# A part of w2 on 64 partitions, loaded by eight transfers of eight rows beside the first eight heads

## The chip, the cores and the metric

The kernel runs on one core of a Trainium2 chip. The metric is device time in microseconds (us), the median of several executions. The core has 16 DMA engines (in the trace, a transfer to 128 partitions closes with 16 tiny packets), and they are what this case is about.

## The reference

It is one decode step: a token of two sequences attends over the last 4096 places of a cache, and beside it runs a small dense layer.

```python
# B=2, Sq=1, D=448, 16 query heads, 8 kv heads, Dh=256, W=4096 of 32768 cached places
# F=1792; all arrays bfloat16
xn = layernorm(x)
q = (xn @ wq)                                   # 448 x 4096
k, v = k_cache[:, :, -W:, :], v_cache[:, :, -W:, :]   # each kv head serves two query heads
o = softmax(q @ k.T * Dh**-0.5) @ v
h = xn @ w1 + b1                                # 448 x 1792
act = h * tanh(softplus(h))                     # Mish
out = x + o @ wo + act @ w2                     # w2 is 1792 x 448, 1.6 MB
```

There are 2 x 8 = 16 "heads" of cache to read, each 2 MB of k and 2 MB of v. With the weights this is 77.67 MB from memory in 188.7 us, and little arithmetic on it.

## The kernel before

All large loads are issued by SyncE (SP) in program order into rotating buffers: four for k, five for v. The dense weights use v buffers before the v tiles do. The parts that the change touches:

```python
b1_sb = consts.tile([1, F], BF16)
nc.scalar.dma_start(out=b1_sb[:, :], in_=B_b1.rearrange("(o f) -> o f", o=1))
# ... cut ...
spread = consts.tile([P, NB, P], BF16)
for b4 in range(NB):                      # 16 small copies, used by experiment e3
    rows = slice(b4 * Q, (b4 + 1) * Q)
    for j in range(NQ):
        nc.vector.tensor_copy(out=spread[rows, b4, j * Q : (j + 1) * Q], in_=ident[rows, rows])
# ... cut ...
def load_dense():
    dense["w1"] = v_tile(NS * HF).rearrange("p (s n) -> p s n", s=NS)
    # ... cut: w1 is loaded ...
    dense["w2"] = v_tile(NX * NF * D).rearrange("p (x c d) -> p x c d", x=NX, c=NF)
    nc.sync.dma_start(                    # NX=2 halves, NF=7 rows of w2 on each of 128 partitions
        out=dense["w2"], in_=B_w2.rearrange("(x q c) d -> q x c d", x=NX, q=P)
    )

def dense_in():                           # h, then Mish, into act_bf
    hT_ps = ps_m.tile([P, NF, NX, Bsz], FP32, tag="m", name="hT_ps")
    for c in range(NF):
        # ... cut: 7 matmuls over w1 and 2 for the bias, for each c ...

def dense_out():                          # act @ w2
    w2_sb = dense.pop("w2")
    for x in range(NX):
        for c in range(NF):
            add(act_bf[:, c, x, :], w2_sb[:, x, c, :])

# ... cut ...
for i in range(NK + KA):                  # NK = 16 heads
    if i + 2 < NK:
        load_k(i + 2)
    if i < NK:
        load_v(i, (0, T) if i < NK - 1 else (0, T // 2, 3 * T // 4, T))
        kvh, b = heads[i]
        if b == Bsz - 1:
            load_wo(kvh, parts=1 if i < NK - 1 else 2)
        # ... cut: two halves of k: transpose, scores, softmax ...
    if i == 0:
        dense_in()
    if i == 1:
        dense_out()
    # ... cut: o = p @ v, @ wo ...
```

The softmax here doesn't subtract the row's maximum and nothing guards it: scores larger than these inputs give would overflow.

## Time and profile before

| | before |
|---|---|
| time, median of the first 3 runs | 190.46 us (190.43 to 190.48) |
| span of the profiled execution | 188.7 us |
| share of the 16 DMA engines' span filled by packets of the main queue | 97.3% |
| TensorE's matmuls, VectorE, ScalarE busy | 76%, 60%, 17% |
| last packet of data ends | 185.03 us |
| last v quarter has landed | 184.27 us |
| output issued | 186.51 us |

The last three rows are times from the start of the span. The strips, the DMA table and the chain of work are shown and read in the prediction. The first line below is from the groups of instructions: VectorE's 32 transposes of k, with busy time and mean nanoseconds, then its idle time before them and what ended it. The other two are from the table of DMA issues: count, size of one, and the median time from issue to landing.

```profile
L364 DVE STREAM_TRANSPOSE kt<-k 128x2048 f32<-128x2048 f32 x32 | 73.4, 2296 | 50.6 <-DMA k<-in_A_k_cache_dram 49.6
...
k<-in_A_k_cache_dram SPq DMA_DIRECT2D x16, 2048.0 KB, 31.5
v<-in_A_v_cache_dram SPq DMA_DIRECT2D x15, 2048.0 KB, 34.8
```

VectorE waits 49.6 us in all for k, so it has time to spare. A tile of k is asked for 31.5 us before it lands, though a head of k and v takes only about 10 us to move: several tiles are queued behind the one that moves. A few issues of SyncE do wait for a free buffer (the longest 6.7 us, for a transpose of k), but the DMA engines have other tiles to move meanwhile.

The strips, which sum up nearly eight thousand packets, do not show that one engine is later than another. For that I took the trace's packet records (start, duration, bytes, queue of each packet), followed the strict chains that they form, and noted when each engine reached the tiny packet that closes a transfer. Such lists of **lateness** (nanoseconds after the first of the 16 engines) are my own working from those records, and stand in ordinary fences.

### The profile page before, as it was taken

Reading aid. Unit: us, or ns where it says so; the run is one execution under the profiler, and the core shown is the slowest. Engines: PE = TensorE matmul, PEld = TensorE weight load, DVE = VectorE, ACT = ScalarE, POOL = GpSimd, SP = SyncE. Lnnn points to the kernel's source line nnn. Section 1 sums busy time; section 2 is a strip of 40 time slices with the busy share of each in tenths; the row PEclk is TensorE's granted clock in tenths of the full one; section 3 lists DMA queues with packets and bytes.
Section 4 is the critical chain, followed back from the end, with each engine's and each line's share of the span. In section 5 each row is a group of like instructions: output and inputs, shape, how many; then the busy total and the mean of one; then the engine's idle time right before and its main releaser. Section 6 shows DMA issues by size and latency. Waiting matters only on the chain.

```text
span 188.7 us, 2944 instructions
## 1 busy us (share of the span) xinstructions
PE 144.1 (76%) x1158; PEld 71.7 (38%) x1158; DVE 113.5 (60%) x195; ACT 32.5 (17%) x82; POOL 27.1 (14%) x139
## 2 busy tenths in 40 slices
PE   0152991788995799869985999769986999597782
PEld 0042390234442345334432434324533443254671
DVE  7805505997919392857649381939376673939401
ACT  2300110112212022111222112202311121211101
POOL 8004430033030022003030203003110300000000
PEclk9999995799999699988999699969998799969955
DMA  6999999999999999999999999999999999999991
GB/s 216 423 432 422 430 430 434 438 431 420 417 441 431 420 416 438 441 427 405 442 434 429 434 420 431 434 431 420 431 431 438 412 432 434 431 441 417 408 394 49
DMA packets 7816, 77.86 MB, mean 413 GB/s; under 512 B 757, under 2 KB 2809, under 8 KB 3322
## 3 DMA queue, kind: packets, MB, share of 16 engines
q1 hardware_dynamic: 7796, 77.66, 97.3%
q8 instruction: 9, 0.15, 0.3%
q14 instruction: 5, 0.04, 0.1%
q10 hardware_dynamic: 6, 0.01, 0.0%
HBM read 77.67 MB, written 0.00 MB: 412 GB/s over the span
## 4 chain that ended last, share of the span: by engine, by line
DMA 82%; DVE 11%; issue 2%; PE 2%; SPq 1%; ACT 0%; ACTq 0%
DMA k<-in_A_k_cache_dram 68%; DMA v<-in_A_v_cache_dram 14%; DVE kt L364 8%; DVE pT L397 2%; PE sc L376 1%; SPq L114 0%; PE psA L214 0%; SPq L338 0%; PE q L479 0%; SPq L280 0%; DVE sums L407 0%; SPq L275 0%; DVE sums L404 0%; DVE den_sb L320 0%; ACT p L386 0%
## 5 line engine op out<-in xcount | busy, mean ns | idle before, releaser
L364 DVE STREAM_TRANSPOSE kt<-k 128x2048 f32<-128x2048 f32 x32 | 73.4, 2296 | 50.6 <-DMA k<-in_A_k_cache_dram 49.6
L376 PE MATMUL sc<-kt,qdiag 128*128 128x512 bf16 x256 | 72.7, 433 | 17.6 <-DVE kt L364 15.8
L376 PEld LDWEIGHTS <-qdiag 128*128 128x128 bf16 x256 | 24.7, 105 | 57.2 <-issue 30.0
L431 PE MATMUL o<-v,pT 128*4 128x512 bf16 x192 | 43.4, 379 | 0.0
L264 POOL COPY qdiag<-qrep 32x8 bf16<-32x8 bf16 x128 | 23.1, 213 | 122.4 <-PE sc L376 107.6
L386 ACT ACTIVATE p<-sc 128x512 bf16<-128x512 f32 x32 | 19.1, 597 | 95.6 <-PE sc L376 93.1
L431 PEld LDWEIGHTS <-pT 128*4 128x4 bf16 x192 | 15.8, 87 | 21.8
L397 DVE STREAM_TRANSPOSE pT<-p 128x512 bf16<-128x512 bf16 x32 | 21.5, 672 | 1.1 <-ACT p L386 1.1
L439 ACT COPY o_sb<-o 4x512 f32<-4x512 f32 x12 | 6.9, 574 | 36.8 <-PE o L431 36.8
L214 PE MATMUL psA<-wo,oT 128*2 128x112 bf16 x128 | 3.8, 245 | 11.0 <-DVE oT L447 11.0
L479 PE MATMUL q<-pT,v 128*128 128x2 bf16 x256 | 7.6, 165 | 1.7 <-DMA v<-in_A_v_cache_dram 1.6
L460 PEld LDWEIGHTS q<-ident_f,o_sb 4*128 4x128 f32 x48 | 6.6, 206 | 5.1 <-issue 5.1
L479 PEld LDWEIGHTS <-v 128*128 128x128 bf16 x256 | 7.3, 101 | 2.0 <-DMA v<-in_A_v_cache_dram 2.0
L414 PEld LDWEIGHTS den<-sums,ones_f 128*128 128x128 f32 x32 | 6.8, 220 | 3.3 <-issue 1.7
L460 PE MATMUL q<-ident_f,o_sb 4*128 4x4 f32 x48 | 7.6, 261 | 0.0
L235 PE MATMUL qT_ps<-xs,v 128*128 128x4 bf16 x112 | 3.3, 166 | 4.8 <-DVE ones L201 2.8
L214 PEld LDWEIGHTS <-oT 128*2 128x2 bf16 x128 | 1.8, 87 | 11.9 <-DVE oT L447 11.7
L386 ACT ACTIVATION_READ_ACCUMULATOR p<-sc 128x1 f32 x32 | 6.2, 194 | 0.0
L177 PE MATMUL xnT_ps<-ident,xn_bf 2*128 2x2 bf16 x7 | 0.5, 167 | 6.3 <-DVE xn_bf L139 6.3
L414 PE MATMUL den<-sums,ones_f 128*128 128x2 f32 x32 | 5.1, 229 | 0.0
L235 PEld LDWEIGHTS <-v 128*128 128x128 bf16 x112 | 3.1, 104 | 5.0 <-issue 3.0
L462 DVE COPY osum<-q 128x4 f32<-128x4 f32 x12 | 1.9, 158 | 3.9 <-PE q L460 3.9
(52 smaller groups left out, 46.5 us busy)
## 6 DMA issues: line engine op xcount, KB each, us to landing
k<-in_A_k_cache_dram SPq DMA_DIRECT2D x16, 2048.0 KB, 31.5
v<-in_A_v_cache_dram SPq DMA_DIRECT2D x15, 2048.0 KB, 34.8
v<-in_B_w_dram SPq DMA_DIRECT2D x2, 1568.0 KB, 21.0
wo<-in_A_wo_dram SPq DMA_DIRECT2D x7, 448.0 KB, 31.5
v<-in_A_wq_dram SPq DMA_DIRECT2D x1, 2048.0 KB
v<-in_A_wq_dram SPq DMA_DIRECT2D x1, 1536.0 KB, 10.8
v<-in_A_v_cache_dram SPq DMA_DIRECT2D x1, 1024.0 KB, 29.1
v<-in_A_v_cache_dram SPq DMA_DIRECT2D x2, 512.0 KB, 27.4
```

What stands on the lines that cost most here:

```text
L214: nc.tensor.matmul(part(n), lhsT=lhsT, rhs=w[:, n * DO : (n + 1) * DO], start=start, stop=stop, tile_position=(0, n * Q), skip_group_check ...
L235: nc.tensor.matmul(qT_ps[:, hh, e, :], lhsT=wq_v[s][:, hh, e, :], rhs=xs[:, s, :, :].rearrange("p x b -> p (x b)"), start=(s == 0), stop=( ...
L264: nc.gpsimd.tensor_copy(out=tv[rows, :, e, j * Q : (j + 1) * Q : HS], in_=qrep[rows, :, h0 : h0 + rep, e, x, b],)
L364: nc.vector.transpose(out=kt[:].bitcast(FP32), in_=k[:, half * TH * Dh : (half + 1) * TH * Dh].bitcast(FP32),)
L376: nc.tensor.matmul(psc[:], lhsT=qdiag[i % NW][:, n * NE + e, :], rhs=ktv[:, n, e, :, :], start=(n == 0 and e == 0), stop=(n == NB - 1 and ...
L386: nc.scalar.activation(out=p_sb[:], in_=psc[:].rearrange("p t c -> p (t c)"), func=ACT.Exp, scale=scale, accum_out=state["rs", i][:, s % N ...
L397: nc.vector.transpose(out=pT[:], in_=p_t.pop(s)[:])
L414: nc.tensor.matmul(den[:], lhsT=ones_f[:], rhs=state.pop(("sums", i))[:], start=True, stop=True)
L431: nc.tensor.matmul(po[:], lhsT=pT_t[i * NH + half][:, uh * NP * Q : (uh + 1) * NP * Q : HS], rhs=v[:, u * NP : (u + 1) * NP, :].rearrange( ...
L439: nc.scalar.copy(out=o_sb[:], in_=po[:])
L460: nc.tensor.transpose(pqv[:, u, c, :], ov[:, u, c, :], ident_f[0:NR, 0:NR])
L479: nc.tensor.matmul(po[:, c, :], lhsT=vv[:, t, c, :], rhs=pTv[:, th, 0:Q:HS], start=(t == 0 and c == 0), stop=(t == T - 1), skip_group_chec ...
```

## The change

The intent, as it can be read from the diff: part of w2 is taken out of the transfer that spreads over 16 engines and given to eight of them, so that those eight carry a little more and the other eight a little less. Six of the seven row groups of each half of w2 stay on 128 partitions (NA = 6). The last 128 rows of each half go, two by two, onto 64 partitions, and come in eight transfers of eight partitions, one beside each of the first eight heads. The eight partitions of a transfer lie four apart.

```diff
-    NF = HF // P
+    PW = P // 2
+    NA = HF // P - 1
+    NF = NA + (HF - P * NA) // PW
 ...
+    w2_rest = consts.tile([PW, NX, NF - NA, D], BF16)
+    def hidden(c):
+        if c < NA:
+            return slice(0, P), slice(c, P * NA, NA)
+        return slice(0, PW), slice(P * NA + c - NA, HF, NF - NA)
 ...  b1 moves into the spare end of w1's v buffer
-        dense["w2"] = v_tile(NX * NF * D).rearrange("p (x c d) -> p x c d", x=NX, c=NF)
+        dense["w2"] = v_tile(NX * NA * D).rearrange("p (x c d) -> p x c d", x=NX, c=NA)
 ...
+    def load_rest(u):
+        q0, j = divmod(u, 4)
+        rows = slice(q0 * Q + j, (q0 + 1) * Q, 4)
+        rest = w2_in[:, P * NA : HF, :].rearrange("x (q c) d -> q x c d", q=PW)
+        nc.sync.dma_start(out=w2_rest[rows, :, :, :], in_=rest[rows, :, :, :])
 ...
         hT_ps = ps_m.tile([P, NF, NX, Bsz], FP32, tag="m", name="hT_ps")
+        nc.vector.memset(hT_ps[:], 0.0)
 ...  the hidden layer's matmuls take rows and columns from hidden(c)
+    def dense_rest():
+        for x in range(NX):
+            for c in range(NA, NF):
+                add(act_bf[0:PW, c, x, :], w2_rest[:, x, c - NA, :])
 ...
+            if i < PW // 8:
+                load_rest(i)
 ...
+        if i == 11:
+            dense_rest()
```

More of the change, by code (lines that the diff above doesn't have):

```diff
@@ L98 @@
     nc.scalar.dma_start(out=x_bf[:, :], in_=A_x.flatten_outer_dims())
-    b1_sb = consts.tile([1, F], BF16)
-    nc.scalar.dma_start(out=b1_sb[:, :], in_=B_b1.rearrange("(o f) -> o f", o=1))
     def v_tile(n):
@@ L270 @@
     act_bf = consts.tile([P, NF, NX, Bsz], BF16)
+    w2_rest = consts.tile([PW, NX, NF - NA, D], BF16)
     dense = {}
+    def hidden(c):
+        if c < NA:
+            return slice(0, P), slice(c, P * NA, NA)
+        return slice(0, PW), slice(P * NA + c - NA, HF, NF - NA)
+    w2_in = B_w2.rearrange("(x f) d -> x f d", x=NX)
     def load_dense():
-        dense["w1"] = v_tile(NS * HF).rearrange("p (s n) -> p s n", s=NS)
+        w = v_tile(NS * HF + F)
+        dense["w1"] = w[:, 0 : NS * HF].rearrange("p (s n) -> p s n", s=NS)
+        dense["b1"] = w[0:1, NS * HF : NS * HF + F]
         nc.sync.dma_start(
@@ L278, in load_dense @@
         )
-        dense["w2"] = v_tile(NX * NF * D).rearrange("p (x c d) -> p x c d", x=NX, c=NF)
+        nc.scalar.dma_start(out=dense["b1"], in_=B_b1.rearrange("(o f) -> o f", o=1))
+        dense["w2"] = v_tile(NX * NA * D).rearrange("p (x c d) -> p x c d", x=NX, c=NA)
         nc.sync.dma_start(
-            out=dense["w2"], in_=B_w2.rearrange("(x q c) d -> q x c d", x=NX, q=P)
-        )
+            out=dense["w2"],
+            in_=w2_in[:, 0 : P * NA, :].rearrange("x (q c) d -> q x c d", q=P),
+        )
+    def load_rest(u):
[3 more added lines that the diff above has]
+        nc.sync.dma_start(out=w2_rest[rows, :, :, :], in_=rest[rows, :, :, :])
     def dense_in():
-        w1_v = dense.pop("w1").rearrange("p s (q c) -> p s c q", c=NF)
-        b1_v = b1_sb[:].rearrange("o (x q c) -> o x c q", x=NX, c=NF)
+        w1, b1 = dense.pop("w1"), dense.pop("b1")
         hT_ps = ps_m.tile([P, NF, NX, Bsz], FP32, tag="m", name="hT_ps")
+        nc.vector.memset(hT_ps[:], 0.0)
         for c in range(NF):
+            rows, cols = hidden(c)
             for s in range(NS):
                 nc.tensor.matmul(
-                    hT_ps[:, c, :, :].rearrange("p x b -> p (x b)"),
-                    lhsT=w1_v[:, s, c, :],
+                    hT_ps[rows, c, :, :].rearrange("p x b -> p (x b)"),
+                    lhsT=w1[:, s, cols],
                     rhs=xs[:, s, :, :].rearrange("p x b -> p (x b)"),
@@ L299, in dense_in @@
                 nc.tensor.matmul(
-                    hT_ps[:, c, x, :],
-                    lhsT=b1_v[:, x, c, :],
+                    hT_ps[rows, c, x, :],
+                    lhsT=b1[:, x * HF + cols.start : x * HF + cols.stop : cols.step],
                     rhs=ones[:, :],
@@ L326, in dense_out @@
         for x in range(NX):
-            for c in range(NF):
+            for c in range(NA):
                 add(act_bf[:, c, x, :], w2_sb[:, x, c, :])
+    def dense_rest():
+        for x in range(NX):
+            for c in range(NA, NF):
+                add(act_bf[0:PW, c, x, :], w2_rest[:, x, c - NA, :])
     NSTEP = len(heads) * NH
```

## The prediction

> **What bounds the kernel now.** I read the page's strips first, then the DMA table, then the chain of work that ended last, then the waits, and last the trace's packet records one by one, because the first four all point at the DMA engines.
>
> ```profile
> PE   0152991788995799869985999769986999597782
> DVE  7805505997919392857649381939376673939401
> DMA  6999999999999999999999999999999999999991
> GB/s 216 423 432 422 430 430 434 438 431 420 417 441 431 420 416 438 441 427 405 442 434 429 434 420 431 434 431 420 431 431 438 412 432 434 431 441 417 408 394 49
> ```
>
> The DMA strip is at nine tenths in 38 of 40 slices and the rate is flat near 430 GB/s; no compute engine is full for long. There is no stretch in which the transfers wait for anyone.
>
> ```profile
> q1 hardware_dynamic: 7796, 77.66, 97.3%
> q8 instruction: 9, 0.15, 0.3%
> q14 instruction: 5, 0.04, 0.1%
> ...
> DMA 82%; DVE 11%; issue 2%; PE 2%; SPq 1%; ACT 0%; ACTq 0%
> ```
>
> 97.3% of 16 engines' whole span is data of the program. The two "instruction" queues look like nothing, but keep them in mind: nine packets of 16 KB and a few of 8 KB, each of which sits on one engine.
>
> The chain of work in order of time, its last part, and the longest wait of VectorE:
>
> ```profile
> 127.28 31.36 DMA k<-in_A_k_cache_dram
> ...
> 158.66 25.61 DMA v<-in_A_v_cache_dram
> 184.27 0.05 issue
> 184.31 0.60 PE q L479 x16
> ...
> 184.94 0.18 DVE oT L447
> ...
> 185.16 0.79 PE psA L214 x15
> ```
>
> ```profile
> DVE kt L364 <- DMA k<-in_A_k_cache_dram: 49.6, 14, 9.0
> ```
>
> So the end is: the last quarter of the last v tile lands at 184.27, then about 2 us of compute and the output. A tile has landed when the last of its DMA engines has delivered, so **the slowest of 16 engines sets the time**, not their mean.
>
> Which engine is slow? The packet records of the trace carry start, duration, size and queue. In the main queue the packets fall into 16 strict chains: a 16384 B packet starts 607 ns after the one before it on its engine (27.0 GB/s). The tiny packets that close a transfer therefore give each engine's lateness, in ns after the first engine. My reading of them:
>
> ```
> at   7.4 us: 0 24 30 63 110 141 149 173 194 195 227 230 284 345 407 594
> at 177.2 us: 0 30 172 345 407 594 | 830 887 | 1483 1529 1561 1567 1614 1642 1647 | 1694
> ```
>
> At first the spread is 0.6 us and its order stays exactly the same until an instruction packet comes. After the 16 KB packet of queue 8 at 17.1 us the engine at 227 is at 1647; after the one at 61.7 us the one at 63 is at 1483, and so on: each such packet costs its engine 1.42 us, and each of the seven so far took a different engine. An eighth, at 180.0 us, moves the engine at 0 to 1422. The 8 KB packets of queue 14 cost 0.5 to 0.9 us; four fell during the loads, and two of those (at 48.7 and 175.7 us) on the same engine, which so became the last of all, at 1694. At the end there are seven early engines (up to 888), eight late ones (1422 to 1647) with one fetch each, and that one at 1694.
>
> [...] The trace agrees for 128 rows (16 closing packets per transfer) and for the one-row bias (one packet, at 5.77 us); no transfer of eight is in it. [...]nine packets of 16384 B for 2338 records on TensorE's two rows, about one per 256. [...] The bias's engine[...] can be followed through its exact start times: it is the one at 345, so it is an early one.
>
> **The change part by part.**
>
> Intent, as I read it: the eight engines that carry one TensorE fetch each are 8 to 15, so let the other eight carry a bit more. Seven engines fit that; the eighth does not.
>
> *Main part of w2.* Still two rows' groups on 128 partitions, 16 packets per engine, but 5376 B in place of 6272 B. A 6272 B packet takes a step of 235 ns (239 in the records less 4 of overlap); in proportion 5376 B is 201. Saved: 16 x 34 = 0.54 us on all 16 engines.
>
> *The rest of w2.* Eight transfers of eight rows, each row two packets of 1792 B. A 1792 B packet steps 70 ns (74 less 4, from wo), a closing packet 6. Added: 8 x (2 x 70 + 6) = 1.17 us on eight engines. Net: **+0.63 us on engines 0 to 7, -0.54 us on 8 to 15**.
>
> *The sum per engine at the end.* If the TensorE-fetched engines are 8 to 15, they fall from at most 1647 to about 1110. The seven early ones rise to 660 to 1520. The engine at 1694 is then in 0 to 7 too and rises to 2325. The maximum goes from 1694 to 2325: 0.63 us later. This does not hang on that guess of the numbering. Only seven engines are early; eight get the extra. So at least one late engine gets it, and the mildest case is the one at 1422, which goes to 2052: still 0.36 us later than 1694. Every assignment of eight engines to these offsets gives +0.36 to +0.63.
>
> *TensorE.* Program order shows 34 rows more: 9 more weight load and matmul pairs for the hidden layer (63 to 72) and 8 for its output (56 to 64). A hidden-layer pair takes (28.6 - 24.0)/63 = 73 ns, the whole under 2 us, in a span in which TensorE's matmul row is 76% busy and waits for VectorE and so for k. Off the path. It does move the fetch boundary: the ninth 16 KB packet, now at 184.98 us just after the loads, comes 34 instructions earlier, at around 183 to 184 us. If it takes engine 0 (345 + 630, then +1420) that ends at 2395, a tenth beyond the other.
>
> *The clearing of the hidden-layer accumulator.* One short VectorE memset, 128x32, but in program order it stands behind the third k transpose, which waits for k until 30.3 us. The hidden-layer matmuls, done at 24.0 to 28.6 us before, now run after about 33.3 us, and VectorE stands for their 72 x 73 ns = 5.3 us. A head costs VectorE about 7 us (two k transposes of 2.3, two p transposes of 0.67, small ones) and a head of k and v arrives every 10.3 us, so it catches up in two heads. k is issued 31.5 us (median) before it lands, so a k issue that comes 5 us later is still early.
>
> *Transfers in flight.* An issue on the SP queue waits for the one eight places before it. With the small ones between, eight places hold five large tiles in place of seven: about 10.5 MB, 24 us at 432 GB/s. The engines still do not run dry.
>
> *SP's own instructions.* Eight more issues. SP's 8 KB instruction packet, at 188.2 us now, may move into the loads: 0.5 to 0.9 us for one engine. On an early one it is hidden; on the slowest it would add in full.
>
> *Moving the bias into the spare end of w1's buffer* changes no bytes. The end of the kernel is untouched.
>
> Sum: 190.46 + 0.63 = 191.09; with some weight for the mild case, 191.05.
>
> **The rivals.**
>
> *A gain of 0.3 to 0.5 us.* If the last engine were one of 8 to 15 and nothing but early engines took the extra, the end would be set by the engine at 888 + 630 = 1518, or 0.2 us earlier: 190.3. For it: the design plainly aims there. Against: the count of seven early engines, unless the fetches land otherwise in the changed kernel.
>
> *The queue runs dry* around 40 to 60 us, since VectorE stands 5.3 us and fewer large tiles are in flight. That would cost up to several us and show as a dip in the DMA strip. Against: 24 us in flight; VectorE waits 49.6 us in all for k, so it has room. Time: 192 to 195.
>
> *A second hit on the slowest engine* by SP's packet: 2325 + 0.7, so 191.8.
>
> *Nothing at all:* the extra is hidden and the time stays within 0.1 us. Against: no engine of the 16 ever idles during the loads.
>
> **Range and chances.** The per-engine sum allows +0.36 to +0.63, a late fetch or SP's packet up to +1.3, an unforeseen shift of the fetches -0.2. I take 190.4 to 191.7 for 8 in 10. Two per cent is 3.8 us, six times the largest term of the sum; only a dry queue could reach it.
>
> **What the changed profile would show.** Right: 16 chains of packets without gaps as before; the closing packets late in the run with eight engines lower by 0.54 and eight higher by 0.63; the last engine at about 2.3 us after the first engine's old mark; the last v quarter landing at about 184.9 in place of 184.27. The hidden layer on TensorE at 33 to 39 us and a VectorE wait for it of some 5 us. Wrong: the transfers of eight rows on other than eight engines; instruction packets at other places or other engines, so that none of the eight is late already; a slice of the DMA strip below nine, which would mean a dry queue; or a last v quarter that lands earlier than 184.27.

The two rows of x came as two packets at once (at 1.67 and 1.68 us). That eight rows go to eight engines was the author's estimate. "0 to 7" are names for the eight engines that were expected to take the extra, "8 to 15" for the others; the records number no engine, and which of them TensorE's packets would take was a guess. Engine 0 is the one that carried the bias. A "fetch" is an instruction packet.

Two statements of it, with their figures from the kernel before. *A tile has landed when the last engine has delivered*: of the 16 closing packets of w1, 15 came at 19.64 to 20.23 us and the last at 21.29, and w1 landed at 21.73. *An issue on the SP queue waits for the one eight places before it*: of the 25 issues of SyncE for which the trace tells that landing, 23 began 0.01 to 0.07 us after it (the other two 3.0 and 6.8 us).

## More of the kernel before

All runs told of here are runs of one core. One of them stood out as slow (194.94 us, one of e1's five); the ratios leave it out, and all others are compared with each other.

## The result, and the profile after

The changed kernel took **191.04 us** (190.90 to 191.16, six runs); the kernel before took 190.47 us (190.39 to 190.74) in the same rounds. The ratio is 1.0028, with a 95% interval of 1.0015 to 1.0041. A ratio here is the mean time of one kernel's fast runs over that of the other's fast runs of the same rounds, so it is not quite the ratio of the medians quoted. The change is a loss of about half a microsecond: small, but outside the noise.

The strips, the DMA table and the shares of the chain, from the page of the changed kernel, in the same order as in the prediction:

```profile
PE   0152920989999899969935999769996999597782
DVE  7805506099979591939448381939376673939401
DMA  6999999999999999999999999999999999999990
GB/s 215 427 440 418 431 433 426 431 431 415 436 426 429 430 422 436 432 433 400 441 443 420 440 422 426 426 433 419 444 426 426 430 426 435 433 426 416 417 384 19
...
q1 hardware_dynamic: 7988, 77.67, 97.1%
q8 instruction: 9, 0.15, 0.3%
q14 instruction: 5, 0.04, 0.1%
...
DMA 84%; DVE 9%; PE 3%; SPq 1%; issue 0%; ACT 0%; ACTq 0%
```

The DMA strip has the same row of nines up to the last slice: no queue ran dry. The bytes are the same to 0.01 MB; only the number of packets grew, by 192. Only the last rate differs by more than 20 GB/s: 19 after, 49 before. The kernel does not move data more slowly; some engine ends later.

The end of the chain of work of the changed kernel (start, duration, what), and the issue of the output from SyncE's timeline:

```profile
159.08 25.83 DMA v<-in_A_v_cache_dram
184.91 0.05 issue
184.96 0.60 PE q L504 x16
...
185.58 0.17 DVE oT L472
...
185.80 0.70 PE psA L214 x15
186.50 0.23 ACT res L586
186.74 0.27 ACTq L614
...
187.04 0.29 SPq L587 DMA_DIRECT2D out_dram<-res  x1
```

The last quarter of v landed at 184.91 us in place of 184.27: **0.64 us later**, and the output followed 2.13 us behind it (2.24 before: the chain's matmuls for wo took 0.70 us in place of 0.79). The last data packet ended at 185.66 us (185.03 before).

What happened to VectorE and the queue, from the waits and the issues of the changed kernel. In the first two lines the columns are total us, number of waits and the longest; in the other two, as before, count, size and time to landing:

```profile
DVE kt L389 <- DMA k<-in_A_k_cache_dram: 43.4, 13, 8.2
DVE h_sb L329 <- PE hT_ps L319: 5.1, 1, 5.1
```

```profile
k<-in_A_k_cache_dram SPq DMA_DIRECT2D x16, 2048.0 KB, 25.7
v<-in_A_v_cache_dram SPq DMA_DIRECT2D x15, 2048.0 KB, 26.2
```

VectorE stood 5.1 us for the hidden layer, once, and then waited 6.2 us less for k: the stall was taken out of its slack. A k tile is now asked for 25.7 us before it lands in place of 31.5, which is still more than two heads ahead.

The lateness of the 16 engines shortly before the end, from the packet records:

```
before, 177.2 us: 0 30 172 345 407 594 | 830 887 | 1483 1529 1561 1567 1614 1642 1647 | 1694
after,  177   us: 0 85 462 | 1500 1508 1527 1560 1590 1626 1806 1852 1935 2033 | 2608 2621 | 2887
```

Following each chain of the changed kernel back to the first transfer shows what it had carried by then:

```
no extra, no instruction packet            0, 85, 462
no extra, one 16 KB (TensorE)              1508, 1527, 1560, 1626, 1852
extra, no instruction packet               1500, 1806
extra, one 8 KB instruction packet         1590, 1935, 2033
extra, one 16 KB (TensorE)                 2608, 2621
extra, two 8 KB (VectorE)                  2887  <- last of all
```

The last is one of the eight that got the extra, and it also carried both of VectorE's instruction packets: at 52 to 54 us and at 175.7 us, 843 ns each. That the 16 KB packets belong to TensorE is read from their count (nine for 2338 records before), and that the 8 KB packets belong to VectorE or SyncE from when they move as those engines' instructions change in number (before, VectorE's two fell after 63 and 189 of its records); the records name no owner.

### The profile page after: what moved, and what is told of

The parts are those of the page before. It is cut to its first block, busy times and chain, and to the rows that moved or that the text cites. A ratio compares the mean times of both kernels' runs of the same rounds, so it can differ in the third digit from the quotient of the medians.

```text
span 189.2 us, 2989 instructions
## 1 busy us (share of the span) xinstructions
PE 143.1 (76%) x1175; PEld 71.4 (38%) x1175; DVE 113.6 (60%) x196; ACT 32.5 (17%) x82; POOL 27.2 (14%) x139
## 4 chain that ended last, share of the span: by engine, by line
DMA 84%; DVE 9%; PE 3%; SPq 1%; issue 0%; ACT 0%; ACTq 0%
DMA k<-in_A_k_cache_dram 70%; DMA v<-in_A_v_cache_dram 14%; DVE kt L389 7%; PE hT_ps L310 2%; DVE pT L422 1%; PE hT_ps L319 1%; SPq L114 0%; PE psA L214 0%; PE q L504 0%; SPq L286 0%; SPq L292 0%; SPq L363 0%; DVE den_sb L340 0%; ACTq L614 0%; ACT u_sb L331 0%
## 5 line engine op out<-in xcount | busy, mean ns | idle before, releaser
L401 PE MATMUL sc<-kt,qdiag 128*128 128x512 bf16 x256 | 70.4, 422 | 11.9 <-DVE kt L389 11.8
L456 PE MATMUL o<-v,pT 128*4 128x512 bf16 x192 | 44.3, 384 | 0.0
L401 PEld LDWEIGHTS <-qdiag 128*128 128x128 bf16 x256 | 24.0, 103 | 49.5 <-issue 21.5
L214 PE MATMUL psA<-wo,oT 128*2 128x112 bf16 x128 | 3.2, 219 | 9.9 <-DVE oT L472 9.9
L310 PE MATMUL hT_ps<-xs,v 128*128 128x4 bf16 (+1 forms) x56 | 4.0, 190 | 8.1 <-DVE hT_ps L306 8.1
L504 PEld LDWEIGHTS <-v 128*128 128x128 bf16 x256 | 7.5, 101 | 2.2 <-DMA v<-in_A_v_cache_dram 2.2
L310 PEld LDWEIGHTS <-v 128*128 128x128 bf16 (+1 forms) x56 | 3.3, 144 | 8.6 <-issue 8.5
## 6 DMA issues: line engine op xcount, KB each, us to landing
k<-in_A_k_cache_dram SPq DMA_DIRECT2D x16, 2048.0 KB, 25.7
```

Of the source, the lines that this page charges most:

```text
L214: nc.tensor.matmul(part(n), lhsT=lhsT, rhs=w[:, n * DO : (n + 1) * DO], start=start, stop=stop, tile_position=(0, n * Q), skip_group_check ...
L310: nc.tensor.matmul(hT_ps[rows, c, :, :].rearrange("p x b -> p (x b)"), lhsT=w1[:, s, cols], rhs=xs[:, s, :, :].rearrange("p x b -> p (x b) ...
L401: nc.tensor.matmul(psc[:], lhsT=qdiag[i % NW][:, n * NE + e, :], rhs=ktv[:, n, e, :, :], start=(n == 0 and e == 0), stop=(n == NB - 1 and ...
L456: nc.tensor.matmul(po[:], lhsT=pT_t[i * NH + half][:, uh * NP * Q : (uh + 1) * NP * Q : HS], rhs=v[:, u * NP : (u + 1) * NP, :].rearrange( ...
L504: nc.tensor.matmul(po[:, c, :], lhsT=vv[:, t, c, :], rhs=pTv[:, th, 0:Q:HS], start=(t == 0 and c == 0), stop=(t == T - 1), skip_group_chec ...
```

## The experiments

Theory A is the per-engine sum of the prediction: the end is set by the slowest engine, the eight small transfers add 1.17 us to eight engines, the smaller main part takes 0.54 us from all 16, and instruction packets decide which engines are already late. Theory B is that something else in the change costs the half microsecond: the hidden layer that now runs later, the memset, the more numerous matmuls, or the small transfers' mere presence in the queue. Some expectations also name a rival C: small packets cost the whole memory path, whichever engine carries them. Ten kernels ran, in three groups that each shared one chip and the runs of the kernel before. All gave correct results. "Engine 0" stands in each run for the engine on which the transfers of one row fall; that it is one engine for all of them was followed in e7 only, and that it is the same one from run to run is the author's estimate.

| run | what it is | us | kernel before | ratio (95%) |
|---|---|---|---|---|
| changed | | 191.04 | 190.47 | 1.0028 (1.0015 to 1.0041) |
| e2 | before + the eight small transfers | 191.56 | 190.55 | 1.0055 (1.0042 to 1.0068) |
| e1 | changed, 16 neighbouring rows each | 192.77 (with the slow run; 192.69 without) | 190.55 | 1.0107 (1.009 to 1.0123) |
| e3 | changed, 16 copies to GpSimd | 191.55 | 190.55 | 1.0053 (1.004 to 1.0066) |
| e4 | changed, 4 neighbouring rows each | 193.70 | 190.55 | 1.0169 (1.0153 to 1.0184) |
| e5 | changed, rest on 128 partitions | 191.16 | 190.53 | 1.0032 (1.002 to 1.0045) |
| e6 | before + 8 small ones on engine 0 | 190.47 | 190.53 | 0.9998 (0.9985 to 1.001) |
| e7 | before + 16 small ones on engine 0 | 190.90 | 190.53 | 1.0024 (1.001 to 1.0038) |
| e8 | changed, 8 neighbouring rows each | 192.33 | 190.53 | 1.0097 (1.0084 to 1.0111) |
| e9 | e5 + six small ones on engine 0 | 190.47 | 190.54 | 0.9997 (0.9983 to 1.001) |
| e10 | before + 2 small ones on engine 0 | 191.03 | 190.54 | 1.003 (1.0018 to 1.0043) |

### e2: the eight transfers alone

The kernel before, with w2 whole as it was, loads the same eight rows, spaced four apart, a second time into a tile that nobody reads. (To make room in SBUF the bias moves into w1's buffer, as in the change.) So the extra is there without the smaller main part, without the memset and without the later hidden layer.

```diff
+    again = consts.tile([PW, NX, 2, D], BF16)
+    def load_again(u):
+        q0, j = divmod(u, 4)
+        rows = slice(q0 * Q + j, (q0 + 1) * Q, 4)
+        w2_in = B_w2.rearrange("(x f) d -> x f d", x=NX)
+        rest = w2_in[:, HF - P : HF, :].rearrange("x (q c) d -> q x c d", q=PW)
+        nc.sync.dma_start(out=again[rows, :, :, :], in_=rest[rows, :, :, :])
 ...
+            if i < 8:
+                load_again(i)
```

> The kernel before with eight extra, useless transfers of eight rows beside the first eight heads into a tile that nobody reads; w2, hidden layer and output as before (only the bias moves into w1's buffer, for room). Theory A: the last engine before (two fetches) is one of the eight and gets 8 x 146 ns = 1.17 us with nothing saved, so 190.47 + 1.17 = 191.64 us. Rival B: the hidden layer isn't moved, only the number of small transfers is as in the changed kernel, so between 190.47 and 191.04. Rival C: 229 KB more over all engines is 0.53 us at 432 GB/s, so 191.0 us.

Measured: 191.56 us, a loss of 1.05 us by the ratio (0.0055 x 190.55). Theory A had 191.64, rival C 191.0. The packets confirm the term: each small transfer put 146 to 147 ns onto eight engines and left eight alone. The difference between e2 and the change is then what the smaller main part gives back, 0.0055 - 0.0028 of 190.5 us, or 0.5 us, against the 0.54 of the sum (the packets of the changed kernel gave 0.53: 16 steps of 33 ns less). So the change is **two terms of opposite sign, and both have the size that the packet durations gave**, within intervals of about a quarter of a microsecond on each ratio. The first of them makes a loss by itself, since e2 has no memset, no later hidden layer and no additional matmuls.

### e5 and e9: the same part of w2 shared by all 16 engines

In e5 most of the change stays (the smaller main part, the memset, the later hidden layer, a separate tile for the rest), but the rest comes in two transfers of 128 rows of 896 B, so that each engine gets its 16th (a transfer of 128 rows closes with 16 packets in the trace of the kernel before). The hidden layer so has seven groups of 128 again and not six of 128 and two of 64: the additional matmuls go too.

```diff
-    NF = NA + (HF - P * NA) // PW
+    NF = NA + 1
-    w2_rest = consts.tile([PW, NX, NF - NA, D], BF16)
+    w2_rest = consts.tile([P, NX, D], BF16)
 ...  hidden(c) and dense_rest() take 128 rows
-    def load_rest(u):
-        ...
+    def load_rest(x):
+        nc.sync.dma_start(out=w2_rest[:, x, :], in_=w2_in[x, P * NA : HF, :])
-            if i < PW // 8:
+            if i < NX:
```

> The changed kernel with the rest of w2 on 128 partitions again (one column group of 128 hidden units, two transfers of 128 rows of 896 B beside the first two heads), so that all 16 engines take the same; VectorE's memset ahead of the hidden layer, and the late use of the rest, are kept. Theory A (slowest engine): each engine saves 0.54 us and takes 2 x (8 x 41 + 6) ns = 0.67 us, so 190.55 + 0.13 = 190.65 us. Rival B (the hidden layer behind the memset, VectorE standing 5 us): it stays at 191.0 to 191.1 us.

Measured: 191.16 us, as theory B had it. But the trace of e5 did not show B's reason. Its last data packet ended at 185.20 us, 0.46 us earlier than in the changed kernel and only 0.17 later than before; most of the loss was not in the loads. It came between the last copy of the result and the issue of the output. Below, from the chain of e5 and from its view of SyncE in order of time: ScalarE is done with its two pieces of the copy at 186.62 (its sequencer's line, ACTq, begins at 186.35 and takes 0.27 us), SyncE issues the output at 187.07.

```profile
186.12 0.23 ACT res L583
186.35 0.27 ACTq L611
...
187.07 0.32 SPq L584 DMA_DIRECT2D out_dram<-res  x1
```

That is 0.45 us after the copy ended. In the kernel before the same step took 0.06 us, as its lines show:

```profile
185.94 0.23 ACT res L557
186.18 0.27 ACTq L585
...
186.51 0.34 SPq L558 DMA_DIRECT2D out_dram<-res  x1
```

The profiled run of e5 was the slowest of its five; its closing barrier was also 0.15 us longer than before.

The packet records hold the next clue. SyncE's own 8 KB instruction packet came at 188.24 us in the kernel before, far behind the output, and at 157.1 us, within the loads, in the changed kernel, which has eight more SyncE issues. In e5, with two more, it came at 187.71 us, close behind the output issue (0.64 us; 1.73 in the kernel before). If the number of SyncE's instructions is what matters, e5 with six more small issues should be free of the delay. That is e9: six transfers of one row of 1792 B, all on engine 0, into a tile that nobody reads.

```diff
+    def load_again(u):
+        r = u // 4 * Q + u % 4
+        nc.sync.dma_start(out=again[r : r + 1, :],
+                          in_=B_w2[2 * u : 2 * u + 2, :].rearrange("(o a) d -> o (a d)", o=1))
 ...
             if i < NX:
                 load_rest(i)
+            elif i < 8:
+                load_again(i)
```

> The run with the rest of w2 on 128 partitions, and six useless one-row transfers of 1792 B[...] beside heads 2 to 7, so that SyncE issues as many transfers as in the changed kernel. If the 0.5 us by which that run missed its sum came from SyncE's own 8 KB instruction packet falling next to the output (187.7 us; its output was issued 0.45 us late and the closing barrier was 0.15 us longer), the packet moves back into the loads: data ends at 185.2 us as there, and 190.65 us. If the 0.5 us came from the hidden layer behind the memset (rival B), which is unchanged: 191.1 us.

Measured: **190.47 us, the time of the kernel before** (ratio 0.9997), though e9 does more than e5. The same views of e9:

```profile
184.45 0.60 PE q L509 x16
...
185.99 0.23 ACT res L593
186.22 0.27 ACTq L621
...
186.53 0.27 SPq L594 DMA_DIRECT2D out_dram<-res  x1
```

The output is issued at 186.53, and the last quarter of v landed at 184.41, as before the change to within 0.15 us. This is the run that settles most of theory B. e9 has the change's smaller main part, memset, later hidden layer (VectorE stood 4.2 us for it, 5.1 in the changed kernel) and eight SyncE issues, and spreads the rest over all engines; it costs nothing. It does not have the change's additional matmuls, which no run tests alone; e2, which lacks them too, shows that the loss does not need them. What remains is that eight engines in place of 16 carry the rest.

### e10: two more SyncE issues alone

To see the half microsecond by which e5 missed its sum by itself, the kernel before got two small transfers of one row (3584 B, one packet on engine 0) and nothing else but the moved bias.

```diff
+    def load_again(u):
 ...  as in e6 below
+            if i < 2:
+                load_again(i)
```

> The kernel before with two useless one-row transfers[...] (eight of them cost nothing), so that SyncE has as many issues as in the run with 128 rows. If SyncE's instruction packet at the output is what costs: about 0.5 us over before, 191.0 us, with an output issue some 0.45 us after ScalarE's last copy. If not: 190.5 us.

Measured: 191.03 us, 0.57 us lost by the ratio for two issues of 0.14 us each (estimated from the packets) on an engine that was early in the kernel before (345 ns). SyncE's packet came at 187.82 us, and the output late again, 0.45 us after ScalarE's part of the copy:

```profile
186.24 0.23 ACT res L569
186.47 0.27 ACTq L597
...
187.19 0.28 SPq L570 DMA_DIRECT2D out_dram<-res  x1
```

The run that was profiled is the slowest of the five (191.30 us): before the copy it was already 0.3 us behind the kernel before (its chain waits for wo, which landed at 185.74 us). The delay behind the copy is apart from that.

Eight such issues cost nothing (e6, next), two cost over half a microsecond. So the number of issues alone is not the cost; what goes with it in e5 and e10 is where SyncE's instruction packet falls (187.71 and 187.82 us, 0.64 and 0.63 us behind the output issue). Shown are the count and the time; that SyncE stands still for this packet is an inference, since the packet record begins after the late issue.

### e6 and e7: one engine loaded, step by step

The bias and the first closing packets had said that engine 0 is an early one. These two runs load it alone: one packet of 3584 B per head, for eight heads (e6) and for all 16 (e7).

```diff
+    def load_again(u):
+        r = u // 4 * Q + u % 4
+        nc.sync.dma_start(out=again[r : r + 1, :],
+                          in_=B_w2[4 * u : 4 * u + 4, :].rearrange("(o a) d -> o (a d)", o=1))
 ...
+            load_again(i)          # e6: for i < 8;  e7: load_again(i % 8), for all 16
```

> The kernel before with eight useless transfers of one row (3584 B) beside the first eight heads[...]. Theory A: that engine is early (345 ns after the first; the last stands at 1694), takes 8 x 142 ns = 1.14 us and is still earlier than the last, so nothing: 190.5 us, as before. Rival B2 (eight more small transfers in the queue leave fewer large ones in flight, or cost by their number): as much as in the run with eight rows, 191.5 us.

> The same with sixteen such transfers, one beside each head. Theory A: 16 x 142 ns = 2.27 us[...] puts it at 2617 ns, 0.92 us behind the engine that was last, so 191.4 us (0.2 either way for the order in which the engines start). A mean-bandwidth theory (57 KB of 77.67 MB more): 190.65 us.

Measured: e6 190.47 us, as expected: about 1.1 us of extra work on an early engine is free. e7 190.90 us: a loss, as expected, but 0.46 us (by the ratio) in place of 0.9. In e7's packets engine 0 was the last of all at the end, by 0.55 us over the second. So the direction is right, and the miss is the start: I had counted engine 0's lateness from 345 ns, the value of the kernel before, and in e7 its chain began at about 170 ns, after a first engine that was itself 0.18 us earlier (its first closing packet came at 7.22 us, at 7.39 in the kernel before). The order in which the engines begin **differs from run to run**: without the bias, engine 0 stood 0 to 0.42 us behind the first engine (e6 and the changed kernel), and no experiment here controls it. A sum per engine is no better than this spread. Together the two runs show the case at one engine: about 1.1 us of extra work cost nothing, and about 2.3 us, which made that engine the last, cost 0.46.

### e3: the second packet of the slowest engine taken away

The last engine of the changed kernel carried both of VectorE's instruction packets. With 16 fewer VectorE instructions the second would come after the loads. The 16 small copies into `spread` were given to GpSimd.

```diff
-            nc.vector.tensor_copy(
+            nc.gpsimd.tensor_copy(
                 out=spread[rows, b4, j * Q : (j + 1) * Q], in_=ident[rows, rows]
             )
```

> The changed kernel with the 16 small copies into the spread matrix at the start given from VectorE to GpSimd. VectorE then has 16 instructions fewer, and its second 8 KB instruction packet (now at 175.7 us, 18 records before VectorE's end) should come after the last data. Theory A: the last engine falls from 2887 to 2044 ns after the first, the next one stands at 2621, so 0.27 us less: 190.77 us. If instruction packets don't matter: 191.04 us.

Measured: 191.55 us, a miss. The packet did move: none falls at 175.7 us any more, and two 8 KB packets come at 189.77 and 190.36, where the span ends. But the end of the data moved by only 0.04 us, to 185.62, because another loaded engine, one with a TensorE packet, stood at 2786 in this run, nearly where the removed one had been. The output was issued at 187.00:

```profile
159.33 25.49 DMA v<-in_A_v_cache_dram
184.87 0.60 PE q L504 x16
...
186.45 0.23 ACT res L586
...
187.00 0.29 SPq L587 DMA_DIRECT2D out_dram<-res  x1
```

The half microsecond was lost behind this line: from the output issue to the end of the span took 2.76 us, and 2.17 in the changed kernel, with VectorE's drain in the closing barrier ending at 189.24 us in place of 188.81. An instruction packet near the very end, as in e5 and e10, would fit, but these packets begin only as the span ends, and e3 does not separate that from the copies' move to GpSimd, so its cause stays open. e3 also shows that the engines just behind the last one leave no gain of note: one had to relieve several of them at once.

### e1, e4 and e8: which rows and how many

If the loss is that only eight engines carry the rest, 16 rows per transfer should cure it, and four should make it worse, provided that each row takes an engine of its own, as the eight rows do in the changed kernel (eight chains longer by 147 ns). So e1 took 16 neighbouring partitions and one half of w2 per transfer, and e4 four neighbouring partitions in 16 transfers.

```diff
 e1
-        q0, j = divmod(u, 4)
-        rows = slice(q0 * Q + j, (q0 + 1) * Q, 4)
-        nc.sync.dma_start(out=w2_rest[rows, :, :, :], in_=rest[rows, :, :, :])
+        g, x = divmod(u, NX)
+        rows = slice(g * 16, (g + 1) * 16)
+        nc.sync.dma_start(out=w2_rest[rows, x, :, :], in_=rest[rows, x, :, :])
 e4
+        for v in (2 * u, 2 * u + 1):
+            rows = slice(v * 4, (v + 1) * 4)
+            nc.sync.dma_start(out=w2_rest[rows, :, :, :], in_=rest[rows, :, :, :])
```

> The changed kernel with the rest of w2 in eight transfers of sixteen rows (one packet of 1792 B per engine and transfer), so that all 16 engines take the same. Theory A (the last of the 16 engines sets the end, and eight of them got 0.63 us more): each engine saves 0.54 us of w2 and takes 8 x (70 + 6) ns = 0.61 us, so 190.47 + 0.07 = 190.54 us. Rival B (the hidden layer behind VectorE's memset, and fewer large tiles in flight): both are unchanged, so it stays at 191.04 us. Rival C (small packets cost the whole memory path): 128 small packets and 128 closing ones against 128 and 64, so 191.04 or a little more.

> The changed kernel with the rest of w2 in sixteen transfers of four rows, [...]each +16 x 146 ns - 0.54 us = +1.80 us, the other twelve -0.54 us. Theory A: if the engine with VectorE's two fetches is among the four, 190.47 + 1.80 = 192.27 us; if it isn't but one with a TensorE fetch is, about 192.0; if none of the four is late before, about 190.9 to 191.0. Rival C: the same bytes and packets, so 191.04 us.

Measured: e1 192.77 us and e4 193.70 us. Both are far beyond what was expected, and e1 goes the wrong way. The rates of e1, from its page, show where:

```profile
GB/s 216 419 442 425 424 430 435 431 391 367 390 418 424 418 419 427 429 427 415 424 425 423 432 407 425 432 435 425 432 435 429 422 425 430 429 439 422 411 393 48
```

At the ninth to eleventh slice the rate falls to 367 GB/s. Among the packet records of 37 to 45 us 129 of 187 large packets took over 640 ns (all but one of them 642 to 726), where the usual one takes 611; in the changed kernel it is one of 206. The large packets beside the small transfers were slower. But I had changed two things in these runs: the number of rows, and their place, since the change's rows lie four partitions apart and mine were neighbours. e8 changes the place alone: eight transfers of eight rows, with the rows side by side. (That they use eight engines too is taken over from the changed kernel.)

```diff
-        q0, j = divmod(u, 4)
-        rows = slice(q0 * Q + j, (q0 + 1) * Q, 4)
+        rows = slice(8 * u, 8 * u + 8)
```

> The changed kernel with the eight rows of each small transfer taken next to each other (8u to 8u+7) in place of every fourth; engines, packets and bytes are the same. If only the load of each engine matters: 191.04 us as the changed kernel. If it also matters on which partitions an engine writes (which would explain why the transfers of sixteen and of four neighbouring rows came out 2.2 and 1.4 us over their sums, with the large packets beside them at up to 720 ns in place of 611): clearly more, about 192 to 193 us, with large packets over 640 ns in the trace.

Measured: 192.33 us, 1.3 us above the change (0.0097 - 0.0028 of 190.5), with the last v quarter landing at 186.03 us. From 5 us on, 80 of e8's 4025 large packets took over 640 ns, and 13 of 4026 in the changed kernel. **The choice of partitions alone is worth more than twice the whole effect of the change.** That the place matters is shown by e8; what makes it matter was not shown, as no record of the trace tells how a partition is reached.

## Why the prediction was right

The time came within 0.01 us of the predicted one. That is partly luck: the sum was 191.09, and the 0.04 us taken off for the mild case, which did not come about, stands in for the 0.1 us by which the end became shorter. It is luck in the account of the last engine too. Followed packet by packet, that engine began 0.20 us earlier in the profiled run of the changed kernel than in that of the kernel before, and its first VectorE packet cost it 0.84 us in place of 0.66; the two, which the prediction took to stay as they were, nearly cancel, and the 0.65 us of w2 (1.18 more for the rest, 0.53 less for the main part) is left. By its steps:

- **What bounds the kernel**: right. The DMA strip stayed full, and where I followed single engines to the end (the changed kernel, e3, e7) the time of the loads was that of the last one.
- **The terms.** A 5376 B packet took a step of 202 ns (estimated 201). A small transfer took 146 to 147 ns on eight engines (146). Of the sums, e2 measured the sum of the eight at 1.05 us (1.17), the smaller main part gave back 0.5 us (0.54).
- **Eight rows use eight engines**: right, as the closing packets show: for each small transfer eight of the 16 chains are longer (by 146 to 147 ns).
- **The guess on numbering**: wrong. I took the engines with TensorE's packets to be 8 to 15. In the changed kernel, of the seven that had one by 177 us, two were among the engines with the extra and five were not. The prediction's second argument did not rest on it, and it held: only seven engines are early, eight get the extra, so at least one late engine gets it.
- **Which engine is last**: right. It is the one with VectorE's two 8 KB packets, and it is among the eight with the extra. In the list it stands at 2887, not 2325, mostly because the list counts from the first engine, which is now 0.56 us earlier (176.68 us, 177.23 before); in absolute time it is the +0.63 of the sum: the last data packet came 0.63 us later, the last v quarter 0.64.
- **The hidden layer behind the memset**: right. It ran from 32.7 us on, VectorE stood 5.1 us for it (5.3), and e9 shows that a stall of 4.2 us there costs nothing.
- **SyncE's packet moves into the loads**: right in the move, to 157.1 us; it fell on an engine that ended at 1590 and was hidden. What I had not seen is that its place beside the output goes with a loss of about half a microsecond by itself (e10).
- **TensorE's ninth packet**: I had it at 183 to 184 us. It came at 184.28, and no new last engine came of it.
- **The end of the kernel is untouched**: nearly. It was 0.1 us shorter, from the matmuls for wo.
- **The rivals**: the gain did not come, since a late engine got the extra. (Its heading says 0.3 to 0.5 us, its own sum 0.2.) The dry queue did not come. The second hit on the slowest engine did not come either, though it was a matter of which engine SyncE's packet took.

What stays open: how the hardware chooses the engine for an instruction packet (no rule was found in the records), why the engines begin in another order in each run, why the place of the rows matters, and whether e3's loss is the instruction packet alone.

## What to carry to other kernels

Here the 16 DMA engines were full from start to end (97%), and the time followed the latest engine (its last packet came 0.63 us later, the output 0.53), not the mean, with the same bytes to 0.01 MB. So in a kernel like this one, before bytes are shifted between engines, list how late each one is, and put the extra only where all its engines are early. The counting argument (eight engines get more, seven are early) can be made before the change is run, even without knowing which engine is which. If a small transfer runs beside large ones, try partitions that lie apart (here worth 1.3 us), and when a tiny edit costs half a microsecond for no reason, look at where the sequencers' instruction packets fall (here the output was issued 0.45 us after the copy in place of 0.06, in e5 and e10).
